# Quarter sums of a group in another order, and the last product of the last group in two tiles

## The chip, the cores and the metric

The kernel runs on one core of one Trainium2 chip. The metric is the device time of one execution in microseconds (us), taken as the median of several runs.

## The reference

The computation is an attention block whose weights are cut off near the row maximum, followed by a block with a norm, two matrix products with a relu between them, and a residual. The attention has 8 batches, 8 heads, 576 positions and 64 features per head; the second block has 512 features and 2048 hidden ones.

```python
scores = q @ k.T / 8
thresh = max(scores, -1) - tau
attn   = softmax(where(scores >= thresh, scores, -1e9))
x      = heads side by side(attn @ v)                    # (8, 576, 512)
mu, var = mean(x, -1), mean((x - mu) ** 2, -1)
xn  = (x - mu) / sqrt(var + 1e-6) * g_ln
out = x + relu(xn @ w_ch1) @ w_ch2                       # (8, 576, 512)
```

## The kernel before

**Groups.** The second block works on 16 groups (`NG`), each 288 positions (`TOK`, half a batch) in feature-major form: 128 partitions by four slices of features (`NK`) by 288 positions. `first_part` (L781) makes the 16 hidden tiles of a group: it multiplies the centred input `xc` with `w1` and stores the relu as `hidden`. The norm's factor `rb` is put off to the end, because the relu lets a positive factor through. While TensorE works on one group, the attention of the next batch runs between its products: scores (L421), their maxima `neg` (L435), exponentials (L449), masks (L456), transposes (L546), and the product with the values (L604, L614).

**The second product in quarters.** From the second group on, `second_quarters` (L844) does the second matrix product with seven products of quarters instead of eight. The rows of the result are two halves i, the positions two halves j of 144 columns (`early`, `late`), and `y11`, `y12`, `y21`, `y22` are the four quarters of the tile `y`. Each quarter product is a `segment` (L880): 64 matmuls of 144 columns on TensorE into one PSUM bank, then one copy by ScalarE (L896), either into `y` or into a tile `part`. The order of the seven is `y11`, `p2`, `p7`, the one with `s2`, `p4`, `p5` and, last, the one with `s4` (`p3`), whose sum goes into `y12` alone.

**Sums around them.** The sums and differences of quarters go to a list `drops` through `later` (L858), and `drip` (L688) lets them out at fixed places of the loop (`second_part`, L993): some at once (`urgent`), some where an engine has room. Each engine executes its instructions in the order in which they were recorded, so that an instruction that waits holds up all that stands behind it on that engine. The quarter sum of `s2`'s product and `y11` is called u2; before, it lies in `y21`, and from it follow `u4` (`y12 = y21 + p5`), `u3` (`y21 += p7`), `22` (`y22 = y21 + p5`), `21` (`y21 += p4`) and, after the last product, `12` (`y12 += p3`). All four sums that follow u2 are let out after `p5`, because the first of them needs `p5`. `finish` (L902) multiplies with `rb` and adds `x`: `done11` for `y11`, `hi` for the lower two slices in one, `done12` for `y12`. Then `store` (L720) transposes each of the four feature slices into a tile `ot` (m = 0 and 1 are the slices of `y11`/`y12`, m = 2 and 3 those of `y21`/`y22`), and `send` (L725) issues four output DMAs for it, each from 32 partitions.

**The last group.** Nothing follows the last group. There `hi`, `done12` and the stores of slices 2 and 3 are let out ahead of the last product, on VectorE, and the last product is multiplied by `rb` straight from PSUM (`times_root`, L876) before it is added to the finished `y12`. The output DMAs of the last group are spread: slice 2 on SyncE's queue (SP), slice 3 on GpSimd's (POOL), and slices 0 and 1 by turns on SP's and ScalarE's (ACT). Each queued DMA of SP and ACT signals one of eight semaphores; a DMA that takes a semaphore again waits until the earlier DMA with the same one has landed. The first DMA of slice 1 on SP takes the semaphore of the first DMA of slice 0 on ACT.

Of the kernel before, what the change touches and what calls it, by code (L numbers as in the profile page):

```python
# [8 lines left out]
F32 = mybir.dt.float32  # L9
# [3 lines left out]
ALU = mybir.AluOpType  # L13
# [5 lines left out]
def kernel(  # L19
# [31 lines left out]
    nc = tc.nc  # L51
# [12 lines left out]
    NG = 2 * B  # L64
# [9 lines left out]
    ffn = ctx.enter_context(tc.tile_pool(name="ffn", bufs=2))  # L74
    ps_sc = ctx.enter_context(tc.tile_pool(name="ps_sc", bufs=1, space=bass.MemoryType.PSUM))
    ps_ff = ctx.enter_context(tc.tile_pool(name="ps_ff", bufs=2, space=bass.MemoryType.PSUM))
# [19 lines left out]
    def product(out, lhsT, rhs, **flags):  # L96


        for h in range(2):
            r = slice(64 * h, 64 * h + 64)  # L100
            nc.tensor.matmul(out[r], lhsT=lhsT[:, r], rhs=rhs, **flags)  # L101
# [25 lines left out]
    def load_v(u):  # L127
# [21 lines left out]
        out=tau_sb, in_=bass.AP(tensor=tau.tensor, offset=tau.offset, ap=[[0, 128], [1, 1]])  # L149
# [5 lines left out]
    for t in v_rest:  # L155
# [10 lines left out]
        out=scl_sb, in0=tau_sb, scalar1=0.0, scalar2=SCALE, op0=ALU.is_ge, op1=ALU.mult  # L166
    )
    nc.vector.tensor_scalar(
        out=low_sb, in0=tau_sb, scalar1=0.0, scalar2=BIG, op0=ALU.is_lt, op1=ALU.mult
    )  # L170
    nc.vector.scalar_tensor_tensor(
        out=low_sb, in0=tau_sb, scalar=-1.0, in1=low_sb, op0=ALU.mult, op1=ALU.subtract
# [492 lines left out]
    def mean_of(g):  # L665
        if banks_taken[0]:
            waiting_mean.append(g)
            return
        means[g] = ps_ff.tile([128, TOK], F32, tag="ff", name="mean")
        product(means[g], lhsT=avg_sb, rhs=sums.pop(g), start=True, stop=True)  # L670
# [15 lines left out]
    aside, stores, drops = [], [], []  # L686

    def drip(room=None, everything=False):  # L688


        urgent = [i for i, d in enumerate(drops) if d[0]]
        n = urgent[-1] + 1 if urgent else 0
        room = dict(room or {})
        while drops:
            _, when, eng, cost, go = drops[0]
            if n <= 0 and not everything:
                if when == now or room.get(eng, 0) < cost:
                    break
                room[eng] -= cost
            drops.pop(0)  # L700
            n -= 1
            go()
# [6 lines left out]
    def run_all(calls):  # L709
        now = calls[:]  # L710
        calls.clear()
        for fn in now:
            fn()
# [6 lines left out]
    def store(eng, g, m, o):  # L720
        ot = ffn.tile([128, TOK], F32, tag="o", bufs=4, name="ot")
        eng.transpose(ot, o)
        stores.append(lambda: send(g, m, ot))

    def send(g, m, ot):  # L725
        b, t = divmod(g, 2)
        for i in range(4):
            f = m * 128 + 32 * i
            eng = nc.sync
            if g == NG - 1:  # L730
                eng = (nc.sync, nc.gpsimd)[m % 2] if m >= HM else (nc.sync, nc.scalar)[i % 2]
            eng.dma_start(
                out=out[b, t * TOK : (t + 1) * TOK, f : f + 32].rearrange(
                    "(n r) c -> r n c", r=32
                ),
                in_=ot[32 * i : 32 * i + 32].rearrange("p (n c) -> p n c", c=32),
            )
# [12 lines left out]
    HT, HD, HM = TOK // 2, ND // 2, NK // 2  # L750
    early, late = slice(0, HT), slice(HT, TOK)
# [92 lines left out]
    def second_quarters(g, rb):  # L844

        s2, s3, s4 = more
        b11, b12 = hidden[:, :HD, early], hidden[:, :HD, late]  # L850
        b21, b22 = hidden[:, HD:, early], hidden[:, HD:, late]
        drip(everything=True)
        y = ffn.tile([128, NK, TOK], F32, tag="sq", bufs=1, name="y")
        part_of = lambda t, i, j: t[:, HM * i : HM * i + HM, (early, late)[j]]
        y11, y12, y21, y22 = (part_of(y, i, j) for i in range(2) for j in range(2))
        done = set()

        def later(*calls, urgent=None):  # L858
            for what, cost, fn, eng, *args in calls:

                def go(what=what, fn=fn, eng=eng, args=args):
                    fn(eng, *args)
                    done.add(what)

                drops.append((urgent, now, eng, cost, go))

        def need(*what):
            while not done.issuperset(what):
                drops.pop(0)[-1]()

        def by_fours(eng, out, in0, in1, op):
            for d in range(0, HD, 4):
                at = (slice(None), slice(d, d + 4))
                eng.tensor_tensor(out=out[at], in0=in0[at], in1=in1[at], op=op)  # L874

        def times_root(out, bank):  # L876
            r = rb[:, late].unsqueeze(1).to_broadcast([128, HM, HT])
            dve.tensor_tensor(out=out, in0=bank, in1=r, op=ALU.mult)

        def segment(weights, rhs, out=None, as_it_is=False):  # L880
            bank = ps_ff.tile([128, HM, HT], F32, tag="ff", name="seg")
            for d in range(HD):
                for m in range(HM):
                    at, end = (d, m), (HD - 1, HM - 1)
                    product(
                        bank[:, m], lhsT=weights[:, m, d], rhs=rhs[:, d],
                        start=at == (0, 0), stop=at == end,
                    )
                    if at != end:
                        yield 2, 0.5  # L890
            if out is None:
                out = ffn.tile([128, HM, HT], F32, tag="part", bufs=4, name="part")
            if as_it_is:
                times_root(out, bank)
            else:
                nc.scalar.copy(out, bank)  # L896
            return out

        def add(eng, out, a, b):
            eng.tensor_tensor(out=out, in0=a, in1=b, op=ALU.add)  # L900

        def finish(eng, i, j=None):  # L902

            cols = slice(None) if j is None else (early, late)[j]
            at = (slice(None), slice(HM * i, HM * i + HM), cols)
            z, x = y[at], groups[g][at]
            r = rb[:, cols].unsqueeze(1).to_broadcast(list(z.shape))
            eng.tensor_tensor(out=z, in0=z, in1=r, op=ALU.mult)
            add(eng, z, z, x)

        dve, pool = nc.vector, nc.gpsimd
        done_by = pool if g < NG - 1 else dve
        later(("t3", 3, by_fours, pool, b12, b22, b12, ALU.subtract), urgent=pool)
        banks_taken[0] = True
        yield from segment(w2[0, 0], b11, y11)
        need("t3")
        later(("t2", 3, by_fours, dve, b11, b11, b12, ALU.add), urgent=dve)
        yield 2, 0.5
        p2 = yield from segment(w2[0, 1], b21)
        need("t2")  # L920
        later(("t4", 3, by_fours, pool, b21, b21, b11, ALU.subtract), urgent=pool)
        yield 2, 0.5
        p7 = yield from segment(s3, b12)
        yield 2, 0.5
        yield from segment(s2, b11, y21)
        need("t4")
        later(("t1", 3, by_fours, dve, b11, b22, b11, ALU.subtract), urgent=dve)
        later(
            ("u2", 1, add, pool, y21, y21, y11), ("11", 1, add, pool, y11, y11, p2),
            ("done11", 2, finish, pool, 0, 0),  # L930
        )
        yield 2, 0.5
        p4 = yield from segment(w2[1, 1], b21)
        yield 2, 0.5
        need("t1", "u2", "11")
        p5 = yield from segment(w2[1, 0], b11)
        later(
            ("u4", 1, add, dve, y12, y21, p5), ("u3", 1, add, dve, y21, y21, p7),
            ("22", 1, add, dve, y22, y21, p5), ("21", 1, add, dve, y21, y21, p4),
            ("hi", 3, finish, done_by, 1),  # L940
        )
        ends_here = g == NG - 1
        if ends_here:
            later(("done12", 2, finish, dve, 0, 1))
            later(*((f"o{m}", 1, store, dve, g, m, y[:, m]) for m in (2, 3)))
        yield 2, 0.5
        last = segment(s4, b22, as_it_is=ends_here)
        for _ in range(12):
            yield next(last)
        banks_taken[0] = False  # L950
        while waiting_mean:
            mean_of(waiting_mean.pop(0))
        p3 = yield from last
        later(("12", 1, add, dve, y12, y12, p3))
        if not ends_here:
            later(("done12", 2, finish, done_by, 0, 1))
        later(
            *((f"o{m}", 1, store, dve, g, m, y[:, m]) for m in ((2, 3, 0, 1) if g < NG - 1 else (0, 1)))
        )
        yield 2, 0.5  # L960

    def ffn_steps(g):
# [73 lines left out]
    else:  # L1036
# [3 lines left out]
        for i in range(ND):  # L1040
            nc.sync.dma_start(
                out=w2_sb[:, :, i],
# [146 lines left out]
```

## Time and profile before

| | |
|---|---|
| median of 3 runs | 1357.76 us (1357.47 to 1358.55) |
| the profiled execution's own time | 1357.61 us |
| its span, first to last instruction | 1355.8 us |
| outside the span | 1.81 us |
| TensorE busy | 1326.8 us, 98% of the span |
| VectorE (DVE) / GpSimd (POOL) / ScalarE (ACT) busy | 874.0 / 615.3 / 470.0 us |
| granted TensorE clock | 0.998 |

The rows of the profile name a line of the kernel, an engine, an operation, and the tiles that it writes and reads. PE is TensorE, and an engine's name with a q is its queue of waits and DMA issues. "[1.20 <-PE seg L101]" behind a row says that the engine idled for 1.20 us before it, and what ended that.

### The profile page before, as it was taken

To read this page: it belongs to the slowest core of one execution; us is meant where nothing else is said; L and a number is where in the kernel's file an instruction comes from. 1 tells how busy PE (TensorE), PEld (TensorE's weight loads), DVE (VectorE), ACT (ScalarE), POOL (GpSimd) and SP (SyncE) were. 2 spreads that over 40 slices of the span, in tenths; PEclk is the share of its full clock that TensorE was granted. 3 is DMA by queue.
4 is the path that set the end of the run, shared out by engine and by line. 5 is a ranking of instruction groups with operands and counts; after the bars stand their busy time and mean duration, and the time that the engine had idled before them with its cause. 6 is when DMAs were issued, how large, how long until landed. Compare 5 with 4: busy or idle time off the path is not lost.

```text
span 1355.8 us, 40852 instructions
## 1 busy us (share of the span) xinstructions
PE 1326.8 (98%) x17616; PEld 1003.3 (74%) x17616; DVE 874.0 (64%) x1531; ACT 470.0 (35%) x1022; POOL 615.3 (45%) x824
## 2 busy tenths in 40 slices
PE   8999999999999999999999999999999999999997
PEld 6766657869687786968778696877869687786967
DVE  7978777666755676666766667556766667665202
ACT  4877432332423323232333323233232323333120
POOL 3554455445444344444534454443444445344312
PEclk9999999999999999999999999999999999999999
DMA  9813464457644775447744576446754376443211
GB/s 172 264 52 98 122 182 148 177 159 183 190 141 142 194 197 167 150 136 183 195 149 151 150 191 180 147 146 188 201 169 150 131 189 178 144 155 131 64 19 19
DMA packets 320996, 206.88 MB, mean 153 GB/s; under 512 B 246896, under 2 KB 278384, under 8 KB 312752
## 3 DMA queue, kind: packets, MB, share of 16 engines
q1 hardware_dynamic: 314704, 203.38, 52.0%
q8 instruction: 138, 2.26, 0.7%
q10 hardware_dynamic: 5952, 0.74, 0.4%
q0 software_dynamic: 160, 0.15, 0.1%
q14 instruction: 42, 0.34, 0.1%
HBM read 120.46 MB, written 83.76 MB: 151 GB/s over the span
## 4 chain that ended last, share of the span: by engine, by line
PE 90%; DVE 3%; ACT 2%; DMA 1%; POOL 1%; issue 1%; SPq 1%; POOLq 0%; DVEq 0%; ACTq 0%
PE p L101 37%; PE seg L101 30%; PE sc L421 10%; PE sc L604 8%; PE sc L614 2%; PE tp L101 1%; ACT e L449 1%; DVE e L456 1%; PE var L101 1%; PE mean L101 1%; SPq L118 0%; DMA x_room<-in_moe_w_ch_dram 0%; ACT em L506 0%; DMA qk_room<-in_q_dram 0%; DVE w L308 0%
## 5 line engine op out<-in xcount | busy, mean ns | idle before, releaser
L101 PE MATMUL p<-xc,w 128*64 128x288 f32 x4096 | 517.4, 408 | 6.8 <-ACT part L896 4.6
L101 PEld LDWEIGHTS p<-xc,w 128*64 128x64 f32 x4096 | 287.4, 137 | 214.4 <-issue 13.5
L435 DVE TENSOR_REDUCE neg<-sc 128x2 f32<-128x1152 f32 x144 | 188.6, 1351 | 280.8 <-PE sc L421 280.2
L472 POOL TENSOR_SCALAR e<-e,den 128x576 f32<-128x576 f32 x252 | 193.6, 780 | 133.5 <-DVE den L461 133.5
L101 PE MATMUL seg<-hidden,w 128*64 128x144 f32 x3840 | 247.9, 287 | 0.0
L101 PEld LDWEIGHTS seg<-hidden,w 128*64 128x64 f32 x3840 | 234.9, 137 | 11.5 <-issue 8.5
L456 DVE SCALAR_TENSOR_TENSOR e<-sc,thr,e 128x576 f32<-128x576 f32 x288 | 221.8, 809 | 16.9 <-POOL thr L439 11.2
L801 ACT ACTIVATE hidden<-p 128x288 f32<-128x288 f32 x256 | 106.6, 417 | 303.6 <-PE p L101 303.6
L439 POOL TENSOR_SCALAR thr<-neg,low_sb 128x2 f32<-128x2 f32 x144 | 41.4, 288 | 374.4 <-DVE neg L435 374.0
L449 ACT ACTIVATE e<-sc,neg 128x576 f32<-128x576 f32 x288 | 197.9, 755 | 2.4 <-DVE neg L435 2.4
L546 DVE STREAM_TRANSPOSE et<-e 128x1152 f32<-128x1152 f32 x112 | 153.4, 1374 | 14.7 <-POOL e L472 14.2
L421 PE MATMUL sc<-kT,qT 64*64 64x384 f32 (+3 forms) x2048 | 139.4, 403 | 3.2 <-DVE e L456 2.2
L604 PE MATMUL sc<-em,v_in 128*64 128x128 f32 (+1 forms) x2368 | 129.4, 263 | 0.0
L604 PEld LDWEIGHTS sc<-em,v_in 128*64 128x64 f32 x2368 | 122.8, 137 | 7.9
L101 PE MATMUL seg<-hidden,stage 128*64 128x144 f32 x1920 | 123.3, 286 | 0.0
L101 PEld LDWEIGHTS seg<-hidden,stage 128*64 128x64 f32 x1920 | 117.6, 137 | 2.9 <-issue 2.9
L627 ACT COPY x<-sc 128x128 f32<-128x128 f32 x120 | 31.7, 266 | 238.8 <-PE sc L421 170.4
L421 PEld LDWEIGHTS sc<-kT,qT 64*64 64x64 f32 x2048 | 76.1, 133 | 44.1 <-issue 21.2
L874 POOL TENSOR_TENSOR hidden<-hidden 128x576 f32<-128x576 f32 x60 | 84.8, 1426 | 52.1 <-ACT hidden L801 42.4
L896 ACT COPY part<-seg 128x288 f32<-128x288 f32 x74 | 29.9, 404 | 190.4 <-PE seg L101 190.0
L874 DVE TENSOR_TENSOR hidden<-hidden 128x576 f32<-128x576 f32 x60 | 51.3, 889 | 51.5 <-PE seg L101 48.5
L101 PE MATMUL seg<-hidden,e 128*64 128x144 f32 x960 | 65.3, 286 | 0.0
(145 smaller groups left out, 1098.9 us busy)
## 6 DMA issues: line engine op xcount, KB each, us to landing
scr<-et SPq DMA_DIRECT2D x63, 1152.0 KB, 4.9
em<-scr SPq DMA_DIRECT2D x63, 1024.0 KB, 5.7
q_in<-in_q_dram SPq DMA_DIRECT2D x124, 72.0 KB, 2.7
out_dram<-ot SPq DMA_DIRECT2D x248, 36.0 KB, 3.8
k_in<-in_k_dram SPq DMA_DIRECT2D x120, 72.0 KB, 3.0
er<-scr SPq DMA_DIRECT2D x126, 64.0 KB, 5.2
v_in<-in_v_dram SPq DMA_DIRECT2D x28, 256.0 KB, 5.5
w<-in_moe_w_ch_dram SPq DMA_DIRECT2D x12, 512.0 KB, 4.8
```

Of the source, the lines that this page charges most:

```text
L101: nc.tensor.matmul(out[r], lhsT=lhsT[:, r], rhs=rhs, **flags)
L421: nc.tensor.matmul(sc[h][64 * i : 64 * i + 64, at : at + n], lhsT=ql[r] if s == HP else qT[r, half, j * 128 + 64 * i : j * 128 + 64 * i + 64],
L435: nc.vector.tensor_reduce(out=neg[:, i], in_=pairs[h], axis=AXL.X, op=ALU.max, negate=True,)
L439: nc.gpsimd.tensor_scalar(out=thr[:, i], in0=neg[:, i], scalar1=-1.0, scalar2=low_sb, op0=ALU.mult, op1=ALU.add,)
L449: nc.scalar.activation(es[:, i], blocks[i], func=AF.Exp, bias=neg[:, i : i + 1])
L456: nc.vector.scalar_tensor_tensor(out=es[:, i], in0=blocks[i], scalar=thr[:, i : i + 1], in1=es[:, i], op0=ALU.is_ge, op1=ALU.mult, accum_o ...
L472: nc.gpsimd.tensor_scalar(out=es[:, i], in0=es[:, i], scalar1=den[:, i : i + 1], scalar2=1.0, op0=ALU.mult, op1=ALU.mult,)
L546: nc.vector.transpose(et[:, :, 64 * h : 64 * h + 64].rearrange("p n (j c) -> p j n c", j=2), es[:, 2 * h : 2 * h + 2].rearrange("p j (n c) ...
L604: nc.tensor.matmul(dst[64 * h : 64 * h + 64], lhsT=vt[:, h, c, :], rhs=pick(em[:, 2 * j : 2 * j + 2, c], h), start=c == 0 and first, stop= ...
L627: nc.scalar.copy(x_of(2 * b + (s > HP))[:, s % (HP + 1), 128 * j : 128 * j + 128], pv[j])
L801: nc.scalar.activation(hidden[:, d], p1, func=AF.Relu)
L874: eng.tensor_tensor(out=out[at], in0=in0[at], in1=in1[at], op=op)
```

## The change

Three things are changed in `second_quarters` and what it calls.

1. In every group u2 is kept in `y12` and no longer in `y21`, and the sums that follow it stand in another order: `u3` goes to `y22` and `21` after it, both let out after `p4`, ahead of `p5`'s product; `22` (`y22 += p5`) and `u4` (`y12 += p5`) come after `p5`. Numbers and sizes of these sums stay the same.
2. In the last group, the joint finish `hi` is split: `done21` for `y21` is let out with the sums after `p4`, and `done22` for `y22` after `p5`, ahead of `done12`.
3. In the last group, the last product is made by `last_tiles`: slice 0's 32 matmuls into one bank, then slice 1's 32 into another, and for each slice by itself the product with `rb`, the addition, the transpose and the sends.

`send` is written anew, with the same queue for every DMA as before.

```diff
@@ send
-                eng = (nc.sync, nc.gpsimd)[m % 2] if m >= HM else (nc.sync, nc.scalar)[i % 2]
+                eng = ((nc.sync, nc.scalar), (nc.sync, nc.scalar), (nc.sync,), (nc.gpsimd,))[m]
+                eng = eng[i % len(eng)]
@@ second_quarters
-        def times_root(out, bank):
-            r = rb[:, late].unsqueeze(1).to_broadcast([128, HM, HT])
-            dve.tensor_tensor(out=out, in0=bank, in1=r, op=ALU.mult)
...
-            if as_it_is:
-                times_root(out, bank)
-            else:
-                nc.scalar.copy(out, bank)
+            nc.scalar.copy(out, bank)
             return out
+
+        def last_tiles(weights, rhs):
+            for m in range(HM):
+                bank = ps_ff.tile([128, HT], F32, tag="ff", name="end")
+                for d in range(HD):
+                    product(
+                        bank, lhsT=weights[:, m, d], rhs=rhs[:, d],
+                        start=d == 0, stop=d == HD - 1,
+                    )
+                    if d < HD - 1:
+                        yield 2, 0.5
+                drip(everything=True)
+                z = ffn.tile([128, HT], F32, tag="part", bufs=4, name="z")
+                dve.tensor_tensor(out=z, in0=bank, in1=rb[:, late], op=ALU.mult)
+                add(dve, y12[:, m], y12[:, m], z)
+                store(dve, g, m, y[:, m])
+                run_all(stores)
+                if m < HM - 1:
+                    yield 2, 0.5
...
-        yield from segment(s2, b11, y21)
+        yield from segment(s2, b11, y12)
         need("t4")
         later(("t1", 3, by_fours, dve, b11, b22, b11, ALU.subtract), urgent=dve)
         later(
-            ("u2", 1, add, pool, y21, y21, y11), ("11", 1, add, pool, y11, y11, p2),
+            ("u2", 1, add, pool, y12, y12, y11), ("11", 1, add, pool, y11, y11, p2),
             ("done11", 2, finish, pool, 0, 0),
         )
         yield 2, 0.5
         p4 = yield from segment(w2[1, 1], b21)
+        later(("u3", 1, add, dve, y22, y12, p7), ("21", 1, add, dve, y21, y22, p4))
+        if ends_here:
+            later(("done21", 2, finish, dve, 1, 0))
         yield 2, 0.5
         need("t1", "u2", "11")
         p5 = yield from segment(w2[1, 0], b11)
-        later(
-            ("u4", 1, add, dve, y12, y21, p5), ("u3", 1, add, dve, y21, y21, p7),
-            ("22", 1, add, dve, y22, y21, p5), ("21", 1, add, dve, y21, y21, p4),
-            ("hi", 3, finish, done_by, 1),
-        )
-        ends_here = g == NG - 1
+        later(("22", 1, add, dve, y22, y22, p5), ("u4", 1, add, dve, y12, y12, p5))
         if ends_here:
-            later(("done12", 2, finish, dve, 0, 1))
-            later(*((f"o{m}", 1, store, dve, g, m, y[:, m]) for m in (2, 3)))
+            later(
+                ("done22", 2, finish, dve, 1, 1), ("done12", 2, finish, dve, 0, 1),
+                *((f"o{m}", 1, store, dve, g, m, y[:, m]) for m in (2, 3)),
+            )
+        else:
+            later(("hi", 3, finish, pool, 1))
         yield 2, 0.5
-        last = segment(s4, b22, as_it_is=ends_here)
+        last = last_tiles(s4, b22) if ends_here else segment(s4, b22)
...
-        later(("12", 1, add, dve, y12, y12, p3))
         if not ends_here:
-            later(("done12", 2, finish, done_by, 0, 1))
-        later(
-            *((f"o{m}", 1, store, dve, g, m, y[:, m]) for m in ((2, 3, 0, 1) if g < NG - 1 else (0, 1)))
-        )
+            later(
+                ("12", 1, add, dve, y12, y12, p3), ("done12", 2, finish, pool, 0, 1),
+                *((f"o{m}", 1, store, dve, g, m, y[:, m]) for m in (2, 3, 0, 1)),
+            )
```

More of the change, by code (lines that the diff above doesn't have):

```diff
@@ L874, in by_fours, with segment @@
                 eng.tensor_tensor(out=out[at], in0=in0[at], in1=in1[at], op=op)
-        def times_root(out, bank):
-            r = rb[:, late].unsqueeze(1).to_broadcast([128, HM, HT])
-            dve.tensor_tensor(out=out, in0=bank, in1=r, op=ALU.mult)
-        def segment(weights, rhs, out=None, as_it_is=False):
+        def segment(weights, rhs, out=None):
             bank = ps_ff.tile([128, HM, HT], F32, tag="ff", name="seg")
@@ L911, in second_quarters @@
         dve, pool = nc.vector, nc.gpsimd
-        done_by = pool if g < NG - 1 else dve
+        ends_here = g == NG - 1
         later(("t3", 3, by_fours, pool, b12, b22, b12, ALU.subtract), urgent=pool)
```

## The prediction

> **What bounds the kernel now.** I read the page first. TensorE is busy 98% of the span and 90% of the chain that ended last, so a VectorE (DVE) change counts only where TensorE waits for DVE, or after TensorE's end.
>
> ```profile
> PE 1326.8 (98%) x17616; PEld 1003.3 (74%) x17616; DVE 874.0 (64%) x1531; ACT 470.0 (35%) x1022; POOL 615.3 (45%) x824
> ```
>
> Next TensorE's own waits. From group 2 on its rows show one idle stretch per two groups, 0.57 us, and what ends it is a ScalarE copy, not DVE:
>
> ```profile
> PE p L101 <- ACT part L896: 4.6, 8, 0.6
> ```
>
> So the stage to read is the tail. The timeline of DVE after `p5`'s copy lands (ScalarE, 1342.46 + 0.40):
>
> ```profile
> 1342.24 4.09 PE L101 MATMUL seg<-hidden,e 128*64 128x144 f32 x64
> 1342.96 1.93 DVE L900 TENSOR_TENSOR y<-y,part 128x288 f32<-128x288 f32 x4 [7.49 <-ACT part L896]
> 1344.93 0.76 DVE L908 TENSOR_TENSOR y<-y,rb 128x576 f32<-128x576 f32 x1
> 1345.72 0.76 DVE L900 TENSOR_TENSOR y<-y,x 128x576 f32<-128x576 f32 x1
> 1346.40 0.45 DVE L908 TENSOR_TENSOR y<-y,rb 128x288 f32<-128x288 f32 x1
> 1346.88 0.46 DVE L900 TENSOR_TENSOR y<-y,x 128x288 f32<-128x288 f32 x1
> 1347.26 0.83 DVE L722 STREAM_TRANSPOSE ot<-y 128x288 f32<-128x288 f32 x2
> 1348.01 0.42 DVE L878 TENSOR_TENSOR part<-seg,rb 128x288 f32<-128x288 f32 x1
> 1348.46 0.46 DVE L900 TENSOR_TENSOR y<-y,part 128x288 f32<-128x288 f32 x1
> 1349.01 0.84 DVE L722 STREAM_TRANSPOSE ot<-y 128x288 f32<-128x288 f32 x2
> ```
>
> The reader is to see that TensorE ends at 1346.33, and that the multiply of its product starts 1.68 us later: DVE, not the last product, is late. It idled 7.49 us beforehand, with two sums among those that follow (`u3`, `21`) that needed nothing of `p5`.
>
> Then the queues' rows, since the end is a landing. In order: ACT's first DMA of slice 0 and its landing, SP's first DMA of slice 1, and SP's waits.
>
> ```profile
> 1349.52 0.34 ACTq L732 DMA_DIRECT2D out_dram<-ot  x1
> DMA to landing us min/median/max: 2.8/2.8/2.8
> 1352.40 0.32 SPq L732 DMA_DIRECT2D out_dram<-ot  x1
> SPq L732 <- DMA out_dram<-ot: 1.8, 1, 1.8
> SPq L1184 <- DMA out_dram<-ot: 1.3, 1, 1.3
> ```
>
> ACT's DMA lands at 1352.32; SP, which stood still 1.8 us, issues 0.08 later because its DMA reuses that semaphore. SP's last DMA goes at 1352.76, takes 1.7 us and lands at 1354.46; the span ends at 1355.8. Slice 1 was transposed by 1349.85, long before. So the end hangs on slice 0 reaching ACT, plus one landing, plus SP's last two DMAs.
>
> **The change part by part.**
>
> *Sums ahead of `p5`, last group.* `u3` and `21` (0.47 each) and `done21` (two of about 0.46) move into the idle 7.49 us: `u3` needs u2 (POOL, done 1336.14), `21` the copy of `p4` (1338.54 + 0.40), so all is over by about 1340.9. Queued behind them is only what waits for `p5` anyway. From 1342.96 to the first transpose there remain `22`, `u4`, `done22` and `done12`: six instructions of 288. Starts from the rows: `22` to `u4` 0.49, to the multiply 0.49, to its add 0.48, to the next multiply 0.38 (a start 0.08 before the other's end, as the add of 1345.72 and the multiply of 1346.40 show), to its add 0.48, to the transpose 0.38. Sum 2.70, against 1347.26 - 1342.96 = 4.30. Slices 2 and 3 come 1.60 earlier, and with them SP's four DMAs of slice 2 (1347.76 to 1346.16) and POOL's four of slice 3.
>
> *The last product in two tiles.* The multiply of slice 0 could start at 1348.01 - 1.60 = 1346.41. TensorE's first tile is over at about 1344.3, its second at 1346.33, so at that place the split takes away no wait at all. What it brings is that slice 0 needs only half-sized instructions. There are no rows of 128x144. Two rows give the slope: 0.758 at 576 and 0.457 at 288, so 0.301 per 288, and 144 take 0.307; the multiply out of PSUM 0.416 - 0.150 = 0.27. Slice 0's transpose starts 0.30 + 0.40 after the multiply instead of 1.00, a gain of 0.30; slice 1's ends 2.2 after it instead of 1.84, 0.4 later relative to it. [...] But slice 1 is not what SP waits for: transposed by 1346.41 + 2.2 = 1348.6, needed at about 1350.5. [...]
>
> TensorE's 64 matmuls stay, with 32 in a row into one bank. Products of `first_part` that accumulate in one bank in a row run at 16 in 1.94 us for 288 columns, the same rate per column as 64 in 3.92 us for 144. The second tile's bank is free once `p5` is copied (1342.86), before about 1344.3. Cost 0; a slower second tile of up to 1 us would still be covered by DVE, which needs it at about 1347.5.
>
> *Queues.* Every DMA of SP, ACT and POOL keeps its place, size, queue and semaphore. ACT's first DMA of slice 0 goes at 1349.52 - 1.60 - 0.30 = 1347.62. With the row's 2.8 us it lands at 1350.42, SP goes on at 1350.50: a gain of 1.90. But the backlog in front of it moved only 1.60:
>
> ```profile
> 1350.40:1352.40 2.00, 0.00 (x0) 0.00 (x0) 0.00 (x0) 0.00 (x0) 0.49 (x1) 0.53 0.90 129
> ```
>
> The DMA engines are 0.90 busy there (the last but one number), so the landing may follow the backlog: a gain of 1.60. [...] I take the middle, 1.75.
>
> *The other groups.* Sums keep number and size. In odd groups the five stand in one block, reordered: 0. In even groups 2 to 12, `u3` and `21` now stand ahead of the centring `xc` and `12` is left alone later, so `xc` starts later:
>
> ```profile
> 1129.44 1.38 DVE L546 STREAM_TRANSPOSE et<-e 128x1152 f32<-128x1152 f32 x1 [0.27 <-POOL e L472]
> 1130.99 1.55 DVE L679 TENSOR_TENSOR xc<-x,mean 128x288 f32<-128x288 f32 x4 [0.17 <-PE mean L101]
> 1135.93 11.86 PE L101 MATMUL p<-xc,w 128*64 128x288 f32 x96
> ```
>
> The transposes end at 1130.82, two sums take 0.96, so `xc` goes at about 1131.8 instead of 1130.99 and ends at 1133.3. TensorE takes it at 1135.93: covered by 2.6 us, price without cover 0.8 a group. In the same groups the fourth output transpose moves ahead of the next `neg`. It waits for POOL's `done12`, and POOL, no longer 0.39 us behind `hi`'s sums, is through about 0.4 earlier; two transposes then end at about 1153.7, `neg` starts at 1153.83 as before. If POOL's gain failed, `neg` would slip 0.4, and the scores that need those banks come over 9 us after the masks end. I take 0. In group 14 both sums fall into a DVE idle of 7.48 us: 0.
>
> **Sum.** The profiled execution took 1357.61 (span 1355.8 and 1.81 outside it); less 1.75 it is 1355.86. The median shown is 0.15 above that execution: 1356.0. About 0.2%, or 2.7 us, is what a measurement of this kernel tells from no change; the gain is 0.13%.
>
> **The rivals.**
>
> *Only part of it arrives.* All 16 output DMAs crowd into a slightly shorter time; if slice 0's landing stretches to 3.3 or 3.7, as two others did, 0.5 to 0.9 of the gain goes and the time is 1356.7. For it: the 0.90. Against: the order and spacing are almost kept. If SP is held by something else, nothing is gained: 1357.7.
>
> [...]
>
> *Slower: `xc` late.* In the six even groups TensorE's next group starts on `xc`. Were the 2.6 us of cover not there, each would lose 0.8 to 1.0, some 5.4 together, less 1.75: 1361.4. It decides only if the next group's first product comes more than 2.6 us sooner after the mean than now; scores and value products lie between them in the trace, in an order that the change does not touch.
>
> *It does not do what it says.* If nothing waits on the two tiles (as I argue), the split is worth 0.3 and the reorder carries the rest; the time is unchanged by which is which.
>
> **How the numbers follow.** Forecast 1356.0, own range 1355.7 to 1356.2: 0.57. Part of it or none, up to 1357.7: 0.27. Landing sooner: 0.11, of which nearly all is over 2.7 us. `xc` late or another stall between groups: 0.05. Range 1355.0 to 1357.4, which leaves most of the last two and the bottom of the second out. Faster by over 0.2%: 0.11. Slower: 0.05. The rest, 0.84, is within 0.2%.
>
> **What would show it.** Right: the first tail transpose at about 1345.7, slice 0's multiply at about 1346.4, ACT's first DMA at 1347.6, SP's last two at 1350.5 to 1350.8, span about 1354.1; TensorE's end unmoved. Wrong: multiply rows of 128x144 that wait for TensorE; SP's standstill ended by slice 1's transpose; idle before `p` ended by DVE `xc`; or a span that moved by over 2.7 us.

## The result, and the profile after

The changed kernel took 1356.28 us, the median of 20 runs (1355.40 to 1358.89), against 1358.0 for the kernel before on the same chip: by the medians 1.72 us less. The ratio of the two sets of runs, which is not that of their medians, is 0.9984, with a 95% interval of 0.9978 to 0.9991: about 2.2 us less, and by the interval between 1.2 and 3.0.

The one profiled execution of the changed kernel is no good witness for that total: it took 1358.89 us, with a span of 1357.1. Its page and its timeline near the start, then the matching VectorE row of the kernel before:

```profile
PE 1329.4 (98%) x17616; PEld 1005.5 (74%) x17616; DVE 871.4 (64%) x1535; ACT 469.9 (35%) x1022; POOL 616.2 (45%) x824
25.79 0.78 DVE L372 STREAM_TRANSPOSE kT<-k_in 128x576 f32<-128x576 f32 x1 [2.78 <-DMA k_in<-in_k_dram]
31.11 0.86 PE L421 MATMUL sc<-kT,qT 64*64 64x384 f32 x4 [1.66 <-DVE e L456]
32.59 3.55 PE L421 MATMUL sc<-kT,qT 64*64 64x384 f32 x28 [0.61 <-DVE e L456]
```

```profile
23.70 0.78 DVE L372 STREAM_TRANSPOSE kT<-k_in 128x576 f32<-128x576 f32 x1 [0.89 <-DMA k_in<-in_k_dram]
```

An input landed 1.9 us later there than in the profile before, and the next 28 score matmuls took 3.55 us in place of 2.16 (the granted clock between 30 and 40 us was 0.83, in the profile before 1.00). By 41 us the execution is 3.5 us behind; it is still exactly that far behind at the end of TensorE's work (1349.83 against 1346.33). So totals of single executions cannot be compared, and I read the tail from the end of TensorE's last product instead. That distance was 1355.8 - 1346.33 = 9.47 us before and is 1357.1 - 1349.83 = 7.27 now: 2.20 less, as the ratio says. (Spans are shown to 0.1 us, so a distance is good to 0.05.)

The timeline of TensorE and VectorE in the tail of the changed kernel (start, duration, instruction, and in brackets what VectorE waited for):

```profile
1345.74 4.09 PE L101 MATMUL end<-hidden,e 128*64 128x144 f32 x64
1346.39 0.83 DVE L915 TENSOR_TENSOR y<-y,part 128x288 f32<-128x288 f32 x2 [2.47 <-ACT part L890]
1347.14 0.45 DVE L923 TENSOR_TENSOR y<-y,rb 128x288 f32<-128x288 f32 x1
1347.62 0.46 DVE L915 TENSOR_TENSOR y<-y,x 128x288 f32<-128x288 f32 x1
1348.00 0.45 DVE L923 TENSOR_TENSOR y<-y,rb 128x288 f32<-128x288 f32 x1
1348.48 0.46 DVE L915 TENSOR_TENSOR y<-y,x 128x288 f32<-128x288 f32 x1
1348.86 0.83 DVE L722 STREAM_TRANSPOSE ot<-y 128x288 f32<-128x288 f32 x2
1349.61 0.27 DVE L907 TENSOR_TENSOR z<-end,rb 128x144 f32<-128x144 f32 x1
1349.92 0.31 DVE L915 TENSOR_TENSOR y<-y,z 128x144 f32<-128x144 f32 x1
1350.32 0.48 DVE L722 STREAM_TRANSPOSE ot<-y 128x288 f32<-128x288 f32 x1
1351.36 0.48 DVE L722 STREAM_TRANSPOSE ot<-y 128x288 f32<-128x288 f32 x1
```

The reader is to see the six instructions between 1346.39 and 1348.86, and that the first tail transpose now stands 0.97 us ahead of TensorE's end, where it stood 0.93 behind. Slice 0's multiply no longer waits for anything but VectorE itself.

The queues: ScalarE's first DMA of slice 0 and its landing, SyncE's last two DMAs (slice 1) and the landing of the second, SyncE's waits, and the load of the DMA engines (last but one number) between.

```profile
1350.83 0.33 ACTq L733 DMA_DIRECT2D out_dram<-ot  x1
DMA to landing us min/median/max: 2.1/2.1/2.1
1352.98 1.34 SPq L733 DMA_DIRECT2D out_dram<-ot  x2
DMA to landing us min/median/max: 2.4/2.4/2.4
SPq L733 <- DMA out_dram<-ot: 0.7, 1, 0.7
SPq L1200 <- DMA out_dram<-ot: 1.4, 1, 1.4
1351.90:1353.90 2.00, 0.00 (x0) 0.00 (x0) 0.00 (x0) 0.00 (x0) 0.60 (x1) 0.77 0.92 123
```

SyncE goes on with slice 1 at 1352.98, 3.15 us after TensorE's end in place of 6.07. That is 2.92 sooner, more than the end gained: the last DMA now takes 2.4 us to land instead of 1.7.

### The profile page after: what moved, and what is told of

Same layout as the page of the kernel before. It is cut to its first block, busy times and chain, and to the rows that moved or that the text cites. A ratio compares the mean times of both kernels' runs of the same rounds, so it can differ in the third digit from the quotient of the medians.

```text
span 1357.1 us, 40876 instructions
## 1 busy us (share of the span) xinstructions
PE 1329.4 (98%) x17616; PEld 1005.5 (74%) x17616; DVE 871.4 (64%) x1535; ACT 469.9 (35%) x1022; POOL 616.2 (45%) x824
## 4 chain that ended last, share of the span: by engine, by line
PE 91%; ACT 3%; DVE 2%; DMA 1%; issue 1%; POOL 1%; SPq 1%; POOLq 0%; DVEq 0%; ACTq 0%
PE p L101 37%; PE seg L101 30%; PE sc L421 10%; PE sc L604 8%; PE sc L614 2%; PE tp L101 1%; ACT e L449 1%; PE warm L101 1%; DVE e L456 1%; PE var L101 1%; SPq L118 1%; PE mean L101 1%; ACT em L506 0%; DMA x_room<-in_moe_w_ch_dram 0%; DVE w L308 0%
## 5 line engine op out<-in xcount | busy, mean ns | idle before, releaser
L811 POOL TENSOR_TENSOR hidden<-hidden 128x288 f32<-128x288 f32 x48 | 38.9, 811 | 54.3 <-ACT hidden L809 51.8
```

Of the source, the lines that this page charges most:

```text
L811: nc.gpsimd.tensor_tensor(out=sq[:, 0], in0=sq[:, 0], in1=sq[:, c], op=ALU.add)
```

## The experiments

Every distance below is from TensorE's end (start of its last row plus 4.09) to the end of the span, in that kernel's own profile.

| kernel | first tail transpose, from TensorE's end | distance | ratio to before (95%) |
|---|---|---|---|
| before | +0.93 | 9.47 | |
| changed | -0.97 | 7.27 | 0.9984 (0.9978 to 0.9991) |
| changed, again | -0.97 | 7.33 | 0.9984 (0.9975 to 0.9993) |
| reorder only | -0.97 | 7.29 | 0.9981 (0.9972 to 0.9990) |
| tiles only | +0.93 | 9.41 | 0.9998 (0.9989 to 1.0007) |
| joint finish | -0.37 | 8.01 | 0.9989 (0.9980 to 0.9998) |
| slice 3 not sent | -0.97 | 6.18 | 0.9977 (0.9968 to 0.9986) |
| slice 2 on two queues | -0.98 | 6.88 | 0.9982 (0.9973 to 0.9990) |
| sums on GpSimd, two tiles | -1.00 | 7.39 | 0.9990 (0.9981 to 0.9998) |
| sums on GpSimd, one bank | -1.00 | 7.22 | 0.9985 (0.9977 to 0.9994) |

**The changed kernel again.** No edit.

> The changed kernel once more, unaltered. It measures how much of what the profile of after shows is the same from one execution to the next. Theory (the gain lies behind TensorE's end): the distance from TensorE's end to the end of the span is 7.3 us again (within 0.3), against 9.5 before, and the ratio to before is 0.998 to 0.999; the 3.5 us by which TensorE ended later in the profile of after lie in the first 46 us and are gone or different here. Rival (the reordered sums delay TensorE between the groups): the 3.5 us come back, and idle of TensorE ended by DVE stands beyond the first 200 us.

Measured: median 1355.7, profiled execution 1355.61 with a span of 1353.8. Its TensorE row and SyncE's waits:

```profile
1342.38 4.09 PE L101 MATMUL end<-hidden,e 128*64 128x144 f32 x64
SPq L733 <- DMA out_dram<-ot: 0.7, 1, 0.7
```

TensorE's end is at 1346.47, 3.4 us sooner than in the first profile, so the 3.5 us were that execution's start. The tail is the same within 0.06 us. That is one repeat, and every other kernel below has one profile, so I don't build on differences of 0.1 to 0.2 us.

**The reorder without the two tiles.** In the lines left out, `segment` can again multiply by `rb` straight from PSUM, as in the kernel before.

```diff
...
-        last = last_tiles(s4, b22) if ends_here else segment(s4, b22)
+        last = segment(s4, b22, as_it_is=ends_here)
...
+        if ends_here:
+            later(
+                ("12", 1, add, dve, y12, y12, p3),
+                *((f"o{m}", 1, store, dve, g, m, y[:, m]) for m in (0, 1)),
+            )
```

> The sums in the new order with the finish in parts, but the last product in one bank with one multiply, one add and then two transposes, as before. Theory (VectorE's queue ahead of the multiply was late, not the last product): the first tail transpose stands about 1.0 us before TensorE's end as in after, ScalarE's first DMA about 0.3 later than in after, the distance from TensorE's end to the end 7.3 to 7.7, the ratio 0.9982 to 0.9990. Rival (the two tiles carry the gain): the distance stays above 9, the ratio at 0.9995 or more.

Measured: 7.29, ratio 0.9981. A gain of the whole size is here, without the two tiles. Its rows of the last product and of the multiply, and SyncE's wait for a landing:

```profile
1342.52 4.09 PE L101 MATMUL seg<-hidden,e 128*64 128x144 f32 x64
1346.73 0.46 DVE L879 TENSOR_TENSOR part<-seg,rb 128x288 f32<-128x288 f32 x1 [0.26 <-PE seg L101]
SPq L733 <- DMA out_dram<-ot: 0.9, 1, 0.9
```

With one bank VectorE does wait for TensorE, 0.26 us, and ScalarE's first DMA goes at 1348.28, 1.67 after TensorE's end in place of 1.00: 0.67 later than with two tiles, where 0.3 had been expected. None of this reaches the end. But the DMAs also have other semaphores here: SyncE's first DMA of slice 1 reuses that of slice 2's third, which has landed by then, and only its last one waits, 0.9 us. So this comparison is not of the tiles alone, and what they add in the new order with the same semaphores is not shown: the later slice 0 and the later wait may cancel. The next two keep the semaphores.

**The two tiles without the reorder.** In the lines left out, `last_tiles` stands as in the change.

```diff
...
-        last = segment(s4, b22, as_it_is=ends_here)
+        last = last_tiles(s4, b22) if ends_here else segment(s4, b22)
```

> The sums in the old order with the joint finish, and only the last product in two tiles, each finished and sent by itself. Theory: the first tail transpose stays 0.9 us behind TensorE's end, slice 0's transpose comes 0.3 us sooner, the distance from TensorE's end to the end is 9.2 (9.0 to 9.5), the ratio 0.9995 to 1.0. Rival (the two tiles carry the gain): the distance is 7.5, the ratio 0.9984.

Measured: 9.41, ratio 0.9998. Its slice 0 multiply, SyncE's first DMA of slice 1, and the landing of that:

```profile
1348.67 0.27 DVE L913 TENSOR_TENSOR z<-end,rb 128x144 f32<-128x144 f32 x1
1352.12 0.32 SPq L732 DMA_DIRECT2D out_dram<-ot  x1
DMA to landing us min/median/max: 2.8/2.8/2.8
```

The small instructions do what was said: ScalarE's first DMA goes 0.29 sooner from TensorE's end, and SyncE continues 0.94 sooner (5.13 after TensorE's end in place of 6.07). Then the DMA takes 2.8 us to land where it took 1.7, and 0.06 us is left. The earlier issue at this place was given back as a longer landing.

**The joint finish of slices 2 and 3.**

```diff
-        if ends_here:
-            later(("done21", 2, finish, dve, 1, 0))
...
-                ("done22", 2, finish, dve, 1, 1), ("done12", 2, finish, dve, 0, 1),
+                ("hi", 3, finish, dve, 1), ("done12", 2, finish, dve, 0, 1),
```

> The changed kernel with the finish of slices 2 and 3 as one multiply and one add of 576 columns after the fifth partial product, as before, in place of the four of 288 of which two run ahead of it. Theory (each DVE instruction on the way to the first tail transpose counts in full): two of 0.76 us replace two of 0.46, so that transpose comes 0.6 us later than in after, and the distance from TensorE's end to the end is 7.9 (7.6 to 8.1), ratio about 0.9988. Rival (the DMA engines' backlog sets the end): the distance stays within 0.2 of 7.3.

Measured: 8.01, 0.7 more than the changed kernel, the first transpose 0.6 later, as the two rows of 576 say:

```profile
1344.49 0.75 DVE L923 TENSOR_TENSOR y<-y,rb 128x576 f32<-128x576 f32 x1
1345.28 0.76 DVE L915 TENSOR_TENSOR y<-y,x 128x576 f32<-128x576 f32 x1
```

So this shift of the first transpose, 0.6 us, reached the end at full size. With the DMAs' semaphores the same throughout, the way from before to after is 9.47, 9.41 (the tiles), 8.01 (the sums ahead of `p5` and the new order of the rest: 1.4) and 7.27 or 7.33 (the finish in parts: 0.7).

**Slice 3 of the last group not sent.**

```diff
     def send(g, m, ot):
+        if g == NG - 1 and m == 3:
+            return
```

> The changed kernel with the four output DMAs of the last group's slice 3 left out (GpSimd's, 144 KB of the 576 KB); the transpose for them stays. Theory (the landings stretch because the 16 output DMAs share the DMA engines): the landings that took 2.0 to 3.4 us in the repeat of the changed kernel fall to 1.6 to 2.2, SyncE's last two from 2.6 to 1.7, and the distance from TensorE's end to the end goes from 7.3 to about 6.2 (6.0 to 6.5). Rival (the order of issue and the reused semaphores set the end, not the load): the landings keep their 2.6 to 3.4 and the distance stays at 7.1 to 7.4.

Measured: 6.18. SyncE's last DMA and its landing, then issues with the size and median landing of one, first here and then in the repeat of the changed kernel:

```profile
1350.33 0.46 SPq L735 DMA_DIRECT2D out_dram<-ot  x1
DMA to landing us min/median/max: 1.7/1.7/1.7
out_dram<-ot SPq DMA_DIRECT2D x8, 36.0 KB, 1.7
out_dram<-ot ACTq DMA_DIRECT2D x4, 36.0 KB, 1.9
```

```profile
out_dram<-ot SPq DMA_DIRECT2D x8, 36.0 KB, 2.2
out_dram<-ot ACTq DMA_DIRECT2D x4, 36.0 KB, 2.9
```

All twelve landings are between 1.6 and 2.2 us, where the repeat of the changed kernel has up to 3.4. So the landings of the changed kernel stretched because of what else was on its way. Four DMAs fewer are worth 1.1 to 1.15 us. An estimate from the DMA engines' busy share between the first output DMA and the last landing (0.63 of 6.47 us in the repeat, 0.53 of 5.51 here) is 4.1 and 2.9 us of work for all 16 together: 1.2 less, about what the end gains. It is not shown whether that is the four DMAs' bytes, their packets, or GpSimd's way of issuing them.

**Slice 2 on two queues.**

```diff
-                eng = ((nc.sync, nc.scalar), (nc.sync, nc.scalar), (nc.sync,), (nc.gpsimd,))[m]
+                eng = ((nc.sync, nc.scalar), (nc.sync, nc.scalar), (nc.sync, nc.scalar), (nc.gpsimd,))[m]
```

> The changed kernel with slice 2's four DMAs of the last group by turns on SyncE and ScalarE, in place of all on SyncE, so that the four are issued in half the time and neither queue meets a reused semaphore in front of a transpose. Theory (the DMA engines set the end, and they stand partly idle while the first DMAs are issued): the end comes 0.3 to 0.6 us nearer, distance 6.7 to 7.0. Rival 1 (SyncE's queue is what is late): distance 6.3 or less. Rival 2 (the engines are full from the first DMA on): distance 7.2 to 7.4.

Measured: 6.88, 0.4 to 0.45 nearer than the changed kernel, as the theory said. The ratio, 0.9982, cannot tell that from the changed kernel. SyncE's waits in its tail, and the load of the DMA engines (last but one number) in the first us after TensorE's end, in the repeat of the changed kernel and here:

```profile
SPq L1200 <- DMA out_dram<-ot: 2.6, 1, 2.6
SPq L733 <- DVE z L907: 0.8, 1, 0.8
1346.47:1347.47 1.00, 0.00 (x1) 0.00 (x0) 0.87 (x4) 0.00 (x0) 0.83 (x2) 1.00 0.32 52
1347.82:1348.82 1.00, 0.00 (x0) 0.00 (x0) 0.87 (x4) 0.00 (x0) 0.84 (x2) 1.00 0.54 85
```

No output DMA stands behind a landing any more (SyncE waits 0.8 us for VectorE, and then 2.6 for the last landings at the end), and SyncE's last DMA is issued at 1350.27, 2.45 us after TensorE's end in place of 3.5. It lands 3.1 us after issue. The DMA engines are busier at once, 0.54 against 0.32, as the theory has it. The edit does two things together, it issues slice 2 on two queues and takes away the semaphore wait, and the 0.4 us is for both. Nor is all of it the landings': the last one comes 5.7 us after TensorE's end (ScalarE's, 1350.34 and 3.2) in place of 5.9 to 6.0, and the other 0.2 lies between it and the end of the span, 1.2 us here and 1.4 in the repeat. No run shows why that part is shorter.

**Two of the sums on GpSimd.**

```diff
-        later(("22", 1, add, dve, y22, y22, p5), ("u4", 1, add, dve, y12, y12, p5))
+        later(("22", 1, add, dve, y22, y22, p5), ("u4", 1, add, pool if ends_here else dve, y12, y12, p5))
...
-                ("done22", 2, finish, dve, 1, 1), ("done12", 2, finish, dve, 0, 1),
+                ("done22", 2, finish, dve, 1, 1), ("done12", 2, finish, pool, 0, 1),
```

> The changed kernel with the last group's u4 and done12 on GpSimd in place of VectorE: three instructions fewer on VectorE ahead of the first tail transpose. Theory (the end follows the first output DMA by about 7.8 us, and VectorE sets when that goes): the first tail transpose comes 1.1 us sooner, 2.0 to 2.1 us before TensorE's end, slice 0's multiply now stands at or before TensorE's end, and the distance is 6.3 to 6.7. Rival (slices 0 and 1, which VectorE cannot have before TensorE's end, set it): distance 7.0 to 7.3.

Measured: first transpose at -1.00, distance 7.39, ratio 0.9990. The transpose did not come sooner. VectorE's and GpSimd's rows:

```profile
1343.27 0.46 DVE L915 TENSOR_TENSOR y<-y,part 128x288 f32<-128x288 f32 x1 [2.48 <-ACT part L890]
1343.76 0.94 DVE L923 TENSOR_TENSOR y<-y,rb 128x288 f32<-128x288 f32 x1
1344.73 0.94 DVE L915 TENSOR_TENSOR y<-y,x 128x288 f32<-128x288 f32 x1
1343.31 1.07 POOL L915 TENSOR_TENSOR y<-y,part 128x288 f32<-128x288 f32 x1 [3.91 <-ACT part L890]
1344.46 0.89 POOL L923 TENSOR_TENSOR y<-y,rb 128x288 f32<-128x288 f32 x1
1345.43 0.90 POOL L915 TENSOR_TENSOR y<-y,x 128x288 f32<-128x288 f32 x1
```

Two of VectorE's three instructions take 0.94 us in place of the 0.45 of the kernel where GpSimd rests, so what left VectorE's queue came back as longer instructions. The theory is thereby not tested on the point that it was made for. Its timed runs have a median of 1356.65, 0.9 more than those of the repeat; the tail of its one profile shows 0.06 to 0.12 of that. The rest stays open; the intervals of the two ratios (0.9981 to 0.9998, and 0.9975 to 0.9993) overlap, so it is not clear of noise.

**The same with one bank.** The edit is that of the reorder alone, on top.

> The same with GpSimd, but the last product in one bank with one multiply and one add. Theory: now the multiply waits for TensorE, by about 1.3 us, slice 0's transpose comes 1.0 to 1.2 after TensorE's end as with the new order alone, and the distance is 6.8 to 7.1, so that the two tiles are worth 0.3 to 0.5 us here, where they are worth nothing without GpSimd's help. Rival (the two tiles are worth nothing in any case): the distance is the same as with GpSimd and two tiles, within 0.15.

Measured: 7.22, and the multiply waits 0.28 us for TensorE, not 1.3, since VectorE was not freed. The multiply, and the only wait of SyncE for landings in the tail:

```profile
1346.70 0.46 DVE L879 TENSOR_TENSOR part<-seg,rb 128x288 f32<-128x288 f32 x1 [0.28 <-PE seg L101]
SPq L1212 <- DMA out_dram<-ot: 2.3, 1, 2.3
```

One bank is not worse than two tiles (7.39). Both statements miss by a little: the theory had 7.1 at most, the rival a difference within 0.15, and it is 0.17. Nor is this of the tiles alone: the DMAs have other semaphores again, and no output DMA of SyncE stands behind a landing, where with GpSimd and two tiles one does for 0.8 us. The situation that the expectation meant, a VectorE that is early, did not arise. Whether the two tiles pay there is left open.

## Why the prediction was right, point by point

The forecast was 1356.0 us with a gain of 1.75 in its own account; the medians give 1.72, the ratio 2.2 (1.2 to 3.0) and the tail of the profile 2.20. The direction, the place (VectorE's queue behind TensorE's end) and the size, under 0.2%, were right, and the interval, whose upper end is 0.9991, tells even this size from no change, which the forecast had doubted. Three of its terms were not right.

1. *TensorE and the other groups: nothing.* Right. The first product of a group far ahead, before and after:

```profile
262.87 1.43 PE L101 MATMUL p<-xc,w 128*64 128x288 f32 x10 [0.57 <-ACT part L896]
266.33 1.92 PE L101 MATMUL p<-xc,w 128*64 128x288 f32 x14 [0.57 <-ACT part L890]
```

From it to the last product, 1342.24 (1345.74), it is 1079.37 us before and 1079.41 after. In the six even groups `xc` did start later, by 0.87 us (in the first of them 343.19, against 338.86 plus 3.46 that the whole execution was behind), as forecast at 0.8, and the product that reads it did not. TensorE's wait for ScalarE's copy is 4.6 us in 8 times, before and after.

2. *Six instructions, 2.70 us from the first to the transpose.* They took 2.47. The term is mis-sized at its first two steps: `22` and `u4` were priced 0.49 and 0.49 apart, from rows in which each sum reads what the one ahead of it wrote (`22` after `u3`) or overwrites what that one read (`u3` after `u4`, `21` after `22`). In the new order it is 0.75 us from the start of `22` to that of `done22`'s multiply, because `u4` reads and writes nothing that `22` writes, nor the multiply anything that `u4` writes. The forecast itself had the price of a start without that dependence, 0.38, from the before profile at 1346.40, and used it only further on. With 0.07 from an earlier start, the transposes came 1.90 sooner, not 1.60.

3. *The two tiles: 0.30, carried to the end.* The step itself was right (0.27 and 0.31 us for the halves against 0.27 and 0.307 forecast; ScalarE's first DMA 0.29 sooner in the tiles-only kernel). The carrying was wrong. The chain was taken as a sum of fixed links: transpose, ScalarE's landing 2.8, SyncE's two DMAs, 1.7. The tiles alone moved SyncE's DMA 0.94 sooner, and the end 0.06. And that no wait would be taken away held only for VectorE's predicted time: being 0.30 earlier than worked out, it would have waited 0.26 for TensorE with one bank.

4. *The landing, 2.8.* Here the row was the wrong choice for the changed kernel: ScalarE's landing took 2.1 and SyncE's standstill fell from 1.8 to 0.7. The chance of 0.11 for "landing sooner" was for a landing shorter than that row and a gain of which nearly all lay over 2.7; no run shows a fixed length of a landing from which that could be worked out, and what the runs showed in its place is that SyncE's eight landings in the tail took 1.6 to 3.3 us before and 1.6 to 3.4 after. A gain of 2.7 or more did not come, for the reason of point 3: SyncE continued 2.92 sooner, and its last landing went from 1.7 to 2.4, so that 2.2 remained.

The two errors of one sign (points 2 and 4: 0.3 and 0.7 us) and that of the other (point 3: 0.7) left 0.45 us. That they came so near to cancelling is luck; for the tiles alone the chain of links gives 0.3, and 0.06 came. What the experiments put in its place: over the kernels with the output sent on the same queues, the end follows the first output DMA (SyncE's first of slice 2) by 8.04 (before), 7.74 and 7.80 (changed), 7.77 (reorder), 7.98 (tiles) and 7.88 us (joint finish). That time is only little changed by when slices 0 and 1 come within it, and falls when a quarter of the output is not sent (1353.2 - 1346.54 = 6.66). So most of the gain is the shift of the first output DMA, 1.90. The other 0.3 (8.04 to 7.74) is not accounted for: kernels that issue in the same order on the same semaphores (changed, tiles, joint finish) differ by 0.24 among themselves. Nor did a run move the first DMA alone: in the joint finish all slices moved together, and with the sums on GpSimd none did.

That slice 1 is not what SyncE waits for was right: it is transposed at 1351.84, and SyncE needs it at 1352.98. ScalarE's queue takes it at once, at 1351.87, but with one bank it would hardly have been there sooner: 2.00 us after TensorE's end in the reorder-only kernel, 2.04 with the tiles.

## What to carry to other kernels

When the end of a kernel is a burst of output DMAs, look for what delays the first of them, and expect a gain of about the shift of that first DMA and all that follows it (here 1.90 us of shift and 2.20 of gain); here instructions made shorter in the middle of the burst, which let SyncE issue 0.94 us sooner, were given back as a landing of 2.8 us in place of 1.7. Sums that do not need the newest partial product belong ahead of it, above all where the engine idles there (7.5 us here), and among those that do need it, an order in which no neighbour reads what the other writes, or overwrites what it reads, started them 0.1 us closer here (0.38 us from one start to the next, in place of 0.49). Compare executions from a mark behind the noisy part, here TensorE's end: the tail repeated to 0.06 us while the starts differed by 3.5.

## What the runs showed of the hardware that was not expected

With two of the sums on GpSimd and the last product in two tiles, two of VectorE's two-input instructions of 288 columns took 0.94 us while GpSimd worked on two-input instructions of its own, against 0.45 in the repeat of the changed kernel, where GpSimd rests. GpSimd's multiply and second add took 0.89 and 0.90, against a mean of 0.80 for each in the changed kernel; its first add took 1.07, the mean of such adds there. The rows read like turns. VectorE's sum of 1343.27, which began first, took its usual 0.46. GpSimd's add ends at 1344.38, VectorE's multiply at 1344.70, GpSimd's multiply at 1345.35, VectorE's add at 1345.67, GpSimd's at 1346.33: each of VectorE's ends comes 0.32 us after GpSimd's, each of GpSimd's 0.65 or 0.66 after VectorE's. No run shows what makes them so. Moving work from VectorE to GpSimd in this stage, where VectorE is late, brought nothing: the first transpose stood at -1.00 in place of -0.97.
